# One tile for the untransposed convolution output, its transposes taken block by block, and two steps of the schedule moved

## The chip, the cores and the metric

The kernel runs on one core of a Trainium2 chip. The time is that of the device, in microseconds, for one launch. One further execution was recorded by the hardware profiler, and every row below comes from it. Engine names are those of the profile: PE (matmul) and PEld (its weight loads), DVE, ACT, POOL, and SP, which here only issues DMAs.

## What is computed

```python
# x: (8, 4160, 192), weight: (8 heads, 7 taps)
w   = softmax(weight, axis=-1)                      # per head
out = causal_conv(x_pad, w)                         # each head's 24 columns, 7 taps back in time
t   = out.reshape(33280, 192)
h   = t @ w_in                                      # 192 -> 1024
solu = h * softmax(h)                               # per token
ln  = (solu - mean(solu)) / sqrt(var(solu) + 1e-6) * g_ln
return ln @ w_out                                   # 1024 -> 192
```

## The kernel before

The 33280 tokens are cut in two ways. For the convolution they form 17 **chunks**, mostly of 2080 tokens (half a batch row). For the rest they form 260 **tiles** of 128 tokens, so that a chunk is 16.25 tiles. From tile 8 on, three tiles make a **step** (`three_steps(i)`, where i is the step's first tile), and steps come in the order 8, 11, 14, and so on to 254. A name such as "step 107" means the step of tiles 107, 108 and 109.

The path of a chunk. SP loads it into `xr`. DVE takes partial maxima (L227), and PE adds them over the partitions by a matmul with ones (`add_up`, L99). From that follows the chunk's scale, and from chunk 4 on POOL splits the scaled values into an upper and a lower half-precision part (`halve_steps`, L282, L286 and L289). PE then convolves two heads at a time (`product_of`, L349), in four **sessions** for each chunk. Each session is evacuated by ACT (`upper_part`, L399) and DVE (`lower_part`, L408) into the untransposed tile `y16`, as three blocks of 128 columns: block 0 holds the upper parts of columns 0 to 127, block 2 their lower parts, and block 1 both parts of the last 64 columns. Every block is cut into two parts by time (slots 0 to 9, and 10 to 18). SP transposes a block's part by DMA into one of four buffers in `pad` (`turn`, L450), POOL copies it from there into `ring` (`pack`, L462 and L467), and block 1 is copied once more within SBUF by a DMA into `ring2` (`double`, L481). A tile of tokens reads `ring` and `ring2` as the stationary operand of its first product.

The path of a tile. PE computes `ph` (L861 and the small products of L884 and L896), DVE scales it and takes its minimum (L931), ACT the exponential (L938), DVE the product (L948), ACT the upper half of the result (L956), and POOL the lower half (L968). SP transposes both into `pT` (L970). The second product (L1000) of a tile runs one step or more after its first: at the start of step i for tile i-5, in its middle for i-4, and at its end for i-3.

Each engine works through its own instructions in the order in which the program emits them, and so does SP's DMA queue. The order is written out by hand in `three_steps`, and a table (`plans`) tells in which step a load, a partial maximum, a session, or a group of transposes is emitted. Transposes and `double` go through the list `moves`, from which `move()` takes one at three places of each step: behind the lower half of the step's first tile, behind that of the second, and at the step's end. A `pack` is emitted at the third `move()` after its transpose.

The untransposed output is a fresh tile for each chunk and part, each in a buffer of its own. A new tile can be written only when everything that reads the old one is done:

```python
if first not in self.y16:
    size = NJM - 2 * PW if first else 2 * PW
    self.y16[first] = yp.tile(
        [P, NB, size, P], F16, name=f"y16_{self.ch}_{first}",
        tag=f"y16_{first > 0}", bufs=1,
    )
```

Of the kernel before, what the change touches and what calls it, by code (L numbers as in the profile page):

```python
# [8 lines left out]
F16 = mybir.dt.float16  # L9
# [11 lines left out]
def kernel(  # L21
# [10 lines left out]
    P = 128  # L32
# [9 lines left out]
    NB = 2 * D // P  # L42
    NT = B * S // P
    FIRST = 1024
    PW = 5
# [21 lines left out]
    NJM = max(-(-n // CW) for _, _, n in spans)  # L67
# [4 lines left out]
    cp = ctx.enter_context(tc.tile_pool(name="cp", bufs=1))  # L72
    xp = ctx.enter_context(tc.tile_pool(name="xp", bufs=1))
    yp = ctx.enter_context(tc.tile_pool(name="yp", bufs=2))
# [52 lines left out]
    class Chunk:  # L127
        def __init__(self, ch):
            self.ch = ch
            self.b, self.t0, self.n = spans[ch]  # L130
            self.exact, self.quarter = ch < 4, ch > 2
            self.nw = -(-self.n // CW)
            slots = NWM if self.quarter else self.nw
            self.cuts = list(range(0, slots, PW)) + [slots]
            self.np = len(self.cuts) - 1
            cut = PW if ch == 1 else min(2 * PW, self.nw)
            self.parts = [(0, cut)] + [(cut, self.nw)] * (cut < self.nw)
            self.y16 = {}
            self.raw = [None] * self.np
            self.sums, self.scaled = 0, False  # L140
            assert not self.quarter or (self.nw == NJM and cut == NWM // 2)
            self.peaks = 2 * self.np if ch < 2 else self.np if ch < 4 else 0
            self.part, self.wide = None, {}
# [216 lines left out]
        def at(self, low, col, z, a, b):  # L360


            blk, c = divmod(col + low * (2 * P if col < P else R), P)
            first = self.part_of(a)
            if first not in self.y16:
                size = NJM - 2 * PW if first else 2 * PW
                self.y16[first] = yp.tile(
                    [P, NB, size, P], F16, name=f"y16_{self.ch}_{first}",
                    tag=f"y16_{first > 0}", bufs=1,
                )  # L370
            rows = slice(0, P if self.quarter else CW)
            return self.y16[first][rows, blk, a - first : b - first, c : c + z - col]

        def part_of(self, a):
            return max(y for y, _ in self.parts if y <= a)

        def cut(self, col, width):

# [54 lines left out]
        def turn(self, blk, a, z):  # L433


            first = self.part_of(a)
            got = self.y16[first][:, blk, a - first : z - first, :]
            if self.quarter:
                at = self.pads % 4 * 10 * P
                Chunk.pads += 1  # L440
                self.wide[blk, a] = pad[:, at : at + (z - a) * P].rearrange(
                    "p (w t) -> p w t", t=P
                )
                to = self.wide[blk, a]
            else:
                at = (self.t0 + a * CW) % RING
                assert at + (z - a) * CW <= RING
                got, to = got[0:CW], ring[:, blk, at : at + (z - a) * CW]
                to = to.rearrange("p (w t) -> p w t", t=CW)
            nc.sync.dma_start_transpose(to, got.rearrange("p w d -> p (w d)"))  # L450
# [45 lines left out]
    ring = cp.tile([P, NB * RING], F16, name="ring")  # L496
    ring = ring.rearrange("p (b t) -> p b t", b=NB)
    ring2 = cp.tile([P, RING], F16, name="ring2")
    pad = cp.tile([P, 4 * NFC * D], F16, name="pad")
    raw_out = pad.bitcast(I32).rearrange("p (f t) -> p f t", t=2)  # L500
    gl = cp.tile([P, NFC], F32, name="gl")
# [174 lines left out]
    for e, bank in enumerate(banks):  # L676
        for q in range(2 * per):
            j = q // 2
# [425 lines left out]
    for ch in range(NCH):  # L1104
        lefts.append(left)
        n = (left + spans[ch][2]) // P
# [26 lines left out]
    def sums(c, a, z):  # L1133
        spread_over(a, z, "sum", [(c, h) for j in range(c.np) for h in c.halves(j)])
# [13 lines left out]
    def plans():  # L1148
        c2, c3, c4, c5 = chunks[2:6]
        for i, a, z in ((8, 0, 2), (11, 2, 6), (14, 6, 8)):  # L1150
            at_tile(i, "conv", *[(c2, hg) for hg in c2.groups()[a:z]])
        assert len(c2.groups()) == 8
        at_tile(11, "open", c2)
        for i, part in zip((11, 14), c2.parts):
            at_tile(i, "turn", *[(c2, (blk, *part)) for blk in (1, 0, 2)])
            at_tile(i, "double", (c2, part))
        sums(c2, 6, 8)
        for j, i in ((2, 5), (3, 6)):
            at_tile(i, "load", (c3, j))
        sums(c3, 8, 14)  # L1160
        for j, i in enumerate((10, 12, 14, 16)):
            at_tile(i, "load", (c4, j))
        sums(c4, 16, 22.4)
        for j, i in enumerate((17, 22, 25, 27)):
            at_tile(i, "load", (c5, j))
        for c in chunks[3:]:
            first = next(t.i for t in tiles if t.ch == c.ch)
            s = first - (first - PAIRED) % 3
            steps = [s + 3 * j - 3 * (c.ch > 4) for j in (-5, -4, -3, -2)]
            for i, hg in zip(steps, c.groups()):  # L1170
                at_tile(i, "conv", (c, hg))
            at_tile(steps[2], "open", c)
            p0, p1 = c.parts
            at_tile(steps[2], "turn", *[
                lambda c=c, q=q: turn_piece(c, *q)
                for q in ((0, *p0), (2, *p0), (0, *p1), (1, *p0), (2, *p1), (1, *p1))
            ])
            if c.ch > 5:
                back = next(t for t in tiles if t.ch == c.ch - 3)
                spread_over(back.i, back.i + 0.6 * back.n, "load", [(c, j) for j in range(c.np)])  # L1180
            if c.ch > 4:
                back = next(t for t in tiles if t.ch == c.ch - 3)
                sums(c, back.i + 0.4 * back.n, back.i + 0.9 * back.n)

    class Queue:

# [21 lines left out]
    def follow(c, i):  # L1208

        chain.extend(  # L1210
            (c.add_up, i + 1 + (c.ch > 1)) if f is None else (f, None)
            for f in c.scale_steps()
        )

        def go():
            c.scaled = True
            if c.exact:
                return
            for j in range(c.np):
                queue.put(c.halve_steps(j, quick=False), (c.ch, j))  # L1220

        chain.append((go, None))
# [41 lines left out]
    early, doubles, squares, late, moves = [], [], [], [], []  # L1264
# [173 lines left out]
    def three_steps(i):  # L1438
# [66 lines left out]
            for k, pc, hg in at(n):  # L1505
                k.lower(pc, *hg)

        def move():

            for q in packs:  # L1510
                q[0] -= 1
            while packs and packs[0][0] < 0:
                packs.pop(0)[1]()
            if moves:
                moves.pop(0)()

        def root_squares():
# [142 lines left out]
        if urgent:  # L1660
            for k, q in work["double"]:
                k.double(*q)
        elif start:
            openings()
            doubles.extend(work.get("double", []))
        else:
            opens()
            if not soon:
                turns()
            move()  # L1670
            doubles.extend(work.get("double", []))
        if i == NT - 6:
            ready(b)
# [96 lines left out]
```

## Time and profile before

| | |
|---|---|
| median of two runs | 1278.4 us (1276.75 and 1280.06) |
| profiled execution | 1279.77 us, of which 1278.1 us are the span of the trace |
| PE busy | 1139.7 us, 89% |
| DVE, ACT, POOL busy | 1010.1 (79%), 992.5 (78%), 966.0 (76%) |
| mean granted clock of PE | 0.965 |
| DMA | 231.86 MB, 181 GB/s on average |

Shares of busy time are averages over the whole span. An engine that works through its queue in order can be idle for a while, although its work is waiting, and then the row that ended the idle time tells what it waited for.

### The profile page before, as it was taken

What the parts mean: (1) busy time and instruction counts of PE and PEld (TensorE: products, weight loads), DVE (VectorE), ACT (ScalarE), POOL (GpSimd) and SP (SyncE); (2) the same over time, 40 slices, a digit from 0 to 9 for tenths busy, and PEclk for the clock granted to TensorE, in tenths of its full rate; (3) what the DMA queues carried; (4) which work ended last, traced back from release to release, by engine and by line L of the source; (5) the groups of instructions that cost most, each with busy time, mean ns of one, the idle gap of its engine ahead of it and who ended that gap; (6) DMA issues with size and microseconds to landing.
All of it is one profiled execution on the core that took longest, in us unless ns stands there. A gap on an engine that the chain in (4) does not pass through costs nothing.

```text
span 1278.1 us, 24666 instructions
## 1 busy us (share of the span) xinstructions
PE 1139.7 (89%) x8710; PEld 669.0 (52%) x8710; DVE 1010.1 (79%) x2035; ACT 992.5 (78%) x1788; POOL 966.0 (76%) x862
## 2 busy tenths in 40 slices
PE   5997985969989799998899989798997989989998
PEld 3663542535545455554556545454554646545556
DVE  8876974867878689896789868598895988778777
ACT  7985864867868688786789868597795979779786
POOL 3643376986969679986898959699795998857674
PEclk9899997988999999999999999899998999999999
DMA  8799785995989989998999979899998998979989
GB/s 234 155 184 185 172 172 117 170 209 113 212 149 208 176 174 212 198 199 162 196 203 193 193 161 201 170 179 207 188 187 166 185 207 165 193 152 173 199 157 178
DMA packets 744548, 231.86 MB, mean 181 GB/s; under 512 B 666592, under 2 KB 743336, under 8 KB 744424
## 3 DMA queue, kind: packets, MB, share of 16 engines
q1 hardware_dynamic: 744424, 230.29, 92.6%
q8 instruction: 68, 1.11, 0.4%
q14 instruction: 56, 0.46, 0.1%
HBM read 34.32 MB, written 25.56 MB: 47 GB/s over the span
## 4 chain that ended last, share of the span: by engine, by line
POOL 35%; PE 27%; issue 19%; DMA 8%; ACT 6%; DVE 4%; SPq 1%; POOLq 0%; ACTq 0%; DVEq 0%
POOL p L968 19%; PE po L1000 12%; PE ph L861 11%; DMA pT<-p 6%; POOL ring L467 4%; POOL xs L289 3%; POOL xr L286 2%; POOL t L1071 2%; POOL xs L282 2%; ACT p L956 2%; ACT sq L960 1%; PE ph L896 1%; ACT e L938 1%; DVE ph L931 1%; PE pc L349 1%
## 5 line engine op out<-in xcount | busy, mean ns | idle before, releaser
L968 POOL TENSOR_TENSOR p<-e,p 128x1024 f16<-128x1024 f32 x257 | 548.0, 2136 | 249.8 <-ACT p L956 248.8
L1000 PE MATMUL po<-ohl,pT 128*128 128x192 f16 (+1 forms) x4264 | 559.3, 288 | 73.3 <-DVE y L408 41.1
L1000 PEld LDWEIGHTS <-pT 128*128 128x128 f16 x4264 | 390.5, 99 | 248.7 <-issue 61.2
L861 PE MATMUL ph<-whi,ring 128*128 128x512 f16 x1548 | 423.7, 383 | 13.2 <-POOL ring L467 10.6
L931 DVE TENSOR_SCALAR_CACHE_REDUCE ph<-ph,cv 128x1024 f32<-128x1024 f32 x248 | 319.2, 1288 | 83.6 <-PE ph L896 53.7
L948 DVE SCALAR_TENSOR_TENSOR e<-ph,cv,e 128x1024 f32<-128x1024 f32 x248 | 317.1, 1278 | 22.0 <-ACT e L938 21.3
L938 ACT ACTIVATE e<-ph,sm 128x1024 f32<-128x1024 f32 x260 | 289.6, 1114 | 55.6 <-DVE ph L931 45.0
L861 PEld LDWEIGHTS <-ring 128*128 128x128 f16 x2064 | 193.7, 99 | 235.5 <-issue 30.7
L956 ACT CAST p<-e 128x1024 f16<-128x1024 f32 x257 | 266.5, 1037 | 37.1 <-DVE e L948 34.4
L960 ACT ACTIVATE sq<-e 128x1024 bf16<-128x1024 f32 x260 | 274.2, 1055 | 0.2
L399 ACT ACTIVATE y<-pc 128x432 f16<-128x432 f32 (+5 forms) x130 | 53.9, 475 | 155.2 <-PE pc L349 90.0
L1010 DVE TENSOR_REDUCE raw<-po 128x192 f32<-128x384 f32 x247 | 136.5, 553 | 31.1 <-PE po L1000 28.7
L861 PE MATMUL ph<-wlo,ring 128*128 128x512 f16 x516 | 155.3, 383 | 0.0
L408 DVE SCALAR_TENSOR_TENSOR y<-pc,y 128x432 f16<-128x432 f32 (+5 forms) x130 | 63.3, 532 | 69.0 <-ACT y L399 65.9
L289 POOL TENSOR_TENSOR xs<-xr,xs 128x960 f16<-128x960 f32 x52 | 104.6, 2012 | 1.4
L467 POOL COPY ring<-pad 128x896 f16<-128x896 f16 (+8 forms) x111 | 89.2, 803 | 1.7 <-DMA pad<-y 1.7
L227 DVE TENSOR_REDUCE xa<-xr 128x1 f32<-128x384 f32 x108 | 67.3, 643 | 5.3 <-DMA xr<-in_x_dram 5.3
L896 PE MATMUL ph<-wlo,ring 64*64 64x512 f16 x672 | 51.2, 393 | 19.2 <-DMA ring<-ring 17.1
L286 POOL TENSOR_SCALAR xr<-xr,s 128x960 f32<-128x960 f32 x52 | 55.5, 1067 | 2.6
L1077 ACT ACTIVATE raw<-raw,t 128x192 f32<-128x192 f32 x127 | 56.5, 448 | 0.0
L282 POOL TENSOR_SCALAR xs<-xr,s 128x960 f16<-128x960 f32 x52 | 55.5, 1067 | 0.0
L1071 POOL TENSOR_TENSOR t<-t,mhalf 128x8 f32<-128x8 f32 (+2 forms) x33 | 53.4, 1618 | 2.6
(154 smaller groups left out, 706.5 us busy)
## 6 DMA issues: line engine op xcount, KB each, us to landing
out_dram<-raw SPq DMA_DIRECT2D x127, 192.0 KB, 3.1
xr<-in_x_dram SPq DMA_DIRECT2D x97, 240.0 KB, 4.0
pT<-p SPq DMA_TRANSPOSE x263, 4.6
xr<-in_x_dram SPq DMA_DIRECT2D x6, 480.0 KB, 4.9
xw<-in_x_dram SPq DMA_DIRECT2D x7, 240.0 KB, 4.2
pad<-in_moe_w_out_dram SPq DMA_DIRECT2D x1, 1536.0 KB
ring<-ring SPq DMA_DIRECT2D x12, 120.0 KB, 3.4
ring<-ring SPq DMA_DIRECT2D x10, 140.0 KB, 3.1
```

What stands on the lines that cost most here:

```text
L282: pool.tensor_scalar(h, r, self.s, 1.0, ALU.mult, ALU.mult)
L289: (2.1 * size + 0.2, lambda: pool.tensor_tensor(xl, r, h, ALU.subtract)),
L467: pool.tensor_copy(ring[:, blk, at : at + n * CW].rearrange("p (w t) -> p w t", t=CW), wide[:, w - a : w - a + n, SKIP : SKIP + CW],)
L861: nc.tensor.matmul(bank, lhs, w[:, r, n * 512 : (n + 1) * 512], start=start and j == 0, stop=stop and j == len(ops) - 1,)
L931: dve.tensor_scalar(t.ph, t.ph, t.cv[:, 0:1], None, ALU.mult, ALU.min, accum_out=t.bias)
L938: act.activation(t.e, t.ph, AF.Exp, bias=t.bias, scale=-1.0, accum_out=grp.z[:, g : g + 1])
L948: dve.scalar_tensor_tensor(t.e, t.ph, t.cv[:, 3:4], t.e, ALU.mult, ALU.mult, accum_out=t.grp.s1[:, t.g : t.g + 1],)
L956: act.copy(t.p16[:, :, 0, :], t.halves)
L960: act.activation(junk, t.e, AF.Square, accum_out=t.grp.s2[:, t.g : t.g + 1])
L968: eng.tensor_tensor(t.p16[:, :, 1, :], t.halves, t.p16[:, :, 0, :], ALU.subtract)
L1000: nc.tensor.matmul(t.po[:, 0:n], t.pT[:, a, :], w, start=j == 0, stop=j == len(ops) - 1)
L1010: dve.tensor_reduce(t.grp.raw[:, t.g, :], t.po[:, 0 : 2 * D].rearrange("p (a d) -> p d a", a=2), AX.X, ALU.add,)
```

## The change

Four things change.

1. `y16` becomes one tile for the whole kernel. Nothing is freed between chunks. An instruction that writes into it waits only for those that read or write the same region (chunk 1's second part is put at slots 10 and up, where it lay apart before).
2. The order of a chunk's six transposes changes from (0, first), (2, first), (0, second), (1, first), (2, second), (1, second) to one in which block 1 comes last in both parts, and the `move()` at a step's end takes two entries of the list instead of one.
3. From chunk 4 on, `add_up` may be emitted three tiles later than before, and the partial maxima are spread over an earlier stretch (for chunk 4 the loads, too).
4. Chunk 3's four sessions go from steps 17, 20, 23 and 26 to steps 20, 23, 23 and 26.

```diff
-            self.y16 = {}
...
-            first = self.part_of(a)
-            if first not in self.y16:
-                size = NJM - 2 * PW if first else 2 * PW
-                self.y16[first] = yp.tile(
-                    [P, NB, size, P], F16, name=f"y16_{self.ch}_{first}",
-                    tag=f"y16_{first > 0}", bufs=1,
-                )
             rows = slice(0, P if self.quarter else CW)
-            return self.y16[first][rows, blk, a - first : b - first, c : c + z - col]
+            return y16[rows, blk, self.slots(a, b), c : c + z - col]
+
+        def slots(self, a, b):
+            return slice(a + 5, b + 5) if self.ch == 1 and a >= PW else slice(a, b)
...
-            first = self.part_of(a)
-            got = self.y16[first][:, blk, a - first : z - first, :]
+            got = y16[:, blk, self.slots(a, z), :]
...
+    y16 = cp.tile([P, NB, NJM, P], F16, name="y16")
...
-        for j, i in enumerate((10, 12, 14, 16)):
+        for j, i in enumerate((9, 11, 12, 13)):
             at_tile(i, "load", (c4, j))
-        sums(c4, 16, 22.4)
+        sums(c4, 15, 20)
...
             steps = [s + 3 * j - 3 * (c.ch > 4) for j in (-5, -4, -3, -2)]
+            if c.ch == 3:
+                steps = [20, 23, 23, 26]
...
-                for q in ((0, *p0), (2, *p0), (0, *p1), (1, *p0), (2, *p1), (1, *p1))
+                for q in ((0, *p0), (2, *p0), (0, *p1), (2, *p1), (1, *p0), (1, *p1))
...
-                sums(c, back.i + 0.4 * back.n, back.i + 0.9 * back.n)
+                sums(c, back.i + 0.35 * back.n, back.i + 0.8 * back.n)
...
-            (c.add_up, i + 1 + (c.ch > 1)) if f is None else (f, None)
+            (c.add_up, i + 1 + (c.ch > 1) + 3 * (c.ch > 3)) if f is None else (f, None)
...
-        def move():
+        def move(n=1):
 
             for q in packs:
                 q[0] -= 1
             while packs and packs[0][0] < 0:
                 packs.pop(0)[1]()
-            if moves:
+            for _ in range(min(n, len(moves))):
                 moves.pop(0)()
...
-            move()
+            move(2)
             doubles.extend(work.get("double", []))
```

What this does to the order is shown at three places. Line numbers of the changed kernel are some eight lower (ACT's evacuation is L391 there, the transposes are L441 and L962, POOL's copies L458 and L453).

The first is ACT at the end of step 107, where chunk 9's first session is evacuated (`pc_9_0_0` and `pc_9_0_1` are its two halves). Before, with what each instruction waits for in brackets:

```order
L938 ACTIVATE e_109_6616,z_104_6304<-ph_109_6523,sm_109_6614 128x1024 [waits DVE_49,Pool_49]
L960 ACTIVATE sq_108_6618,s2_104_6306<-e_108_6547 128x1024 [waits Activation_49]
L956 CAST p16_109_6625<-e_109_6616 128x2x512 [waits DMAHW2_49,DVE_49]
L1077 ACTIVATE raw_96_6141<-raw_96_6141,t2_96_5763 128x192
L399 ACTIVATE y16_9_0_6714<-pc_9_0_0_6678 128x10x48 [waits DMAHW3_49,DMAHW5_49,DMAHW0_49,PE_49]
L399 ACTIVATE y16_9_10_6716<-pc_9_0_1_6679 128x9x48 [waits DMAHW2_49,DMAHW3_49,DMAHW0_49,PE_49]
```

And now:

```order
L952 ACTIVATE sq_108_6602,s2_104_6285<-e_108_6527 128x1024 [waits Activation_49]
L262 ACTIVATE xa_10_6183<-xa_10_6183 128x8 [waits DVE_49]
L948 CAST p16_109_6613<-e_109_6600 128x2x512 [waits DMAHW3_49,DVE_49]
L1069 ACTIVATE raw_96_6118<-raw_96_6118,t2_96_5743 128x192 [waits Pool_49]
L391 ACTIVATE y16_76<-pc_9_0_0_6673 128x10x48 [waits PE_49]
L391 ACTIVATE y16_76<-pc_9_0_1_6674 128x9x48 [waits DMAHW1_49,PE_49]
```

Both writes waited for several DMAs, those of all three blocks of chunk 8; now the first of them waits for no DMA, and the second for one, which transposed block 0.

The second place is SP from tile 70 to tile 77, where chunk 6 is transposed (`pad` is the target, `pT` belongs to tiles, `ring2` to `double`). Before:

```order
L970 DMA_TRANSPOSE pT_72_4531<-p16_72_4528 128x16x128
L450 DMA_TRANSPOSE pad_76<-y16_6_10_3914 128x9x128
L970 DMA_TRANSPOSE pT_73_4579<-p16_73_4571 128x16x128
L450 DMA_TRANSPOSE pad_76<-y16_6_0_3912 128x10x128
L1090 DMA out_0_dram<-raw_56_3818 128x2x192
L970 DMA_TRANSPOSE pT_74_4643<-p16_74_4640 128x16x128
L450 DMA_TRANSPOSE pad_76<-y16_6_10_3914 128x9x128
L970 DMA_TRANSPOSE pT_75_4673<-p16_75_4670 128x16x128
L450 DMA_TRANSPOSE pad_76<-y16_6_10_3914 128x9x128
L970 DMA_TRANSPOSE pT_76_4716<-p16_76_4713 128x16x128
L481 DMA ring2_75<-ring_74 64x1120
```

And now:

```order
L962 DMA_TRANSPOSE pT_72_4515<-p16_72_4512 128x16x128
L441 DMA_TRANSPOSE pad_77<-y16_76 128x9x128
L962 DMA_TRANSPOSE pT_73_4563<-p16_73_4555 128x16x128
L441 DMA_TRANSPOSE pad_77<-y16_76 128x10x128
L441 DMA_TRANSPOSE pad_77<-y16_76 128x9x128
L1082 DMA out_0_dram<-raw_56_3809 128x2x192
L962 DMA_TRANSPOSE pT_74_4629<-p16_74_4626 128x16x128
L962 DMA_TRANSPOSE pT_75_4659<-p16_75_4656 128x16x128
L962 DMA_TRANSPOSE pT_76_4706<-p16_76_4703 128x16x128
L472 DMA ring2_75<-ring_74 64x1120
L472 DMA ring2_75<-ring_74 64x960
```

The last two transposes stood behind those of tiles 74 and 75, in the step before the next chunk's first session; now all six stand ahead of tile 74's.

The third place is POOL from tile 106 to tile 108, where chunk 9's last piece is split while chunk 8 is packed (`xr_9_3` and `xs_9` belong to the split, `ring` to the packs, `p16` to tiles). Before:

```order
L286 TENSOR_SCALAR xr_9_3_5278<-xr_9_3_5278,s_9_5750 128x960
L968 TENSOR_TENSOR p16_106_6485<-e_106_6475,p16_106_6485 128x2x512
L467 COPY ring_74<-pad_76 128x1120
L289 TENSOR_TENSOR xs_9_5896<-xr_9_3_5278,xs_9_5896 128x960
L968 TENSOR_TENSOR p16_107_6550<-e_107_6543,p16_107_6550 128x2x512
```

And now:

```order
L960 TENSOR_TENSOR p16_106_6459<-e_106_6449,p16_106_6459 128x2x512
L458 COPY ring_74<-pad_77 128x1120 x2
L281 TENSOR_SCALAR xs_9_6046<-xr_9_3_5259,s_9_5730 128x960
L960 TENSOR_TENSOR p16_107_6530<-e_107_6523,p16_107_6530 128x2x512
L458 COPY ring_74<-pad_77 128x224
L453 COPY ring_74<-pad_77 128x96
L453 COPY ring_74<-pad_77 128x16
L458 COPY ring_74<-pad_77 128x560
L453 COPY ring_74<-pad_77 128x64
L285 TENSOR_SCALAR xr_9_3_5259<-xr_9_3_5259,s_9_5730 128x960
L288 TENSOR_TENSOR xs_9_6046<-xr_9_3_5259,xs_9_6046 128x960
```

The last instruction of the split moved from ahead of tile 107's lower half to behind it, and two more packs stand ahead of it. That holds for chunks 9, 11, 14 and 16, whose `add_up` moved by a step; the other chunks' splits stand where they stood.

## Rows read from the trace of the kernel before

**Rows 1.** Waits, whole span: engine, line, waited for: us in total, times, longest.

```profile
ACT y L399 <- DMA pad<-y: 63.4, 9, 8.8
...
PEld L1000 <- DMA pT<-p: 41.8, 32, 3.1
PE po L1000 <- DVE y L408: 41.1, 11, 7.4
...
ACT y L399 <- DMA ring<-y: 10.8, 1, 10.8
...
PEld po L99 <- ACT xa L263: 9.1, 5, 2.7
```

**Rows 2.** Timeline of ACT in step 107: start, us, what, idle time before it and releaser.

```profile
581.76 0.57 ACT L399 ACTIVATE y<-pc 128x480 f16<-128x480 f32 x1 [1.40 <-PE pc L349]
590.95 0.53 ACT L399 ACTIVATE y<-pc 128x432 f16<-128x432 f32 x1 [8.63 <-DMA pad<-y]
...
591.48 1.11 ACT L938 ACTIVATE e<-ph,sm 128x1024 f32<-128x1024 f32 x1
```

**Rows 3.** Timeline of SP, the same stretch.

```profile
582.60 2.30 SPq L450 DMA_TRANSPOSE pad<-y  x1
...
587.78 1.36 SPq L450 DMA_TRANSPOSE pad<-y  x1
```

**Rows 4.** Timeline of PE, the same stretch.

```profile
580.93 0.78 PE L349 MATMUL pc<-xs,bands 64*64 64x240 f16 x24
...
592.18 5.39 PE L1000 MATMUL po<-ohl,pT 128*128 128x384 f16 x32 [4.95 <-DVE y L408]
```

**Rows 5.** Windows: two steps about a chunk's first session, seven chunks: stretch, us, busy, clock.

```profile
345.30:377.30 32.00, 27.14 (x219) 15.57 (x218) 22.02 (x43) 21.12 (x38) 22.38 (x25) 0.95 0.90 173
...
sum 241.70, PE 192.93 PEld 110.53 DVE 155.37 ACT 148.64 POOL 161.56; mean PE 27.56 PEld 15.79 DVE 22.20 ACT 21.23 POOL 23.08
```

**Rows 6.** The same for the four chunks whose first session comes a step later.

```profile
504.40:531.20 26.80, 25.14 (x218) 15.01 (x217) 22.39 (x48) 21.39 (x38) 24.24 (x27) 1.00 1.05 205
...
sum 108.10, PE 100.87 PEld 60.04 DVE 89.84 ACT 86.05 POOL 85.54; mean PE 25.22 PEld 15.01 DVE 22.46 ACT 21.51 POOL 21.38
```

**Rows 7.** Windows: steps 47 to 230, one quiet step, one stretch of transposes (last: DMA share, GB/s).

```profile
292.60:1159.70 867.10, 796.06 (x6270) 461.83 (x6269) 700.04 (x1394) 686.77 (x1237) 715.18 (x636) 0.98 0.95 183
479.40:491.70 12.30, 12.30 (x82) 6.96 (x80) 11.70 (x23) 12.16 (x25) 11.80 (x11) 1.00 1.09 205
943.60:974.40 30.80, 23.80 (x178) 13.36 (x177) 18.05 (x37) 16.16 (x27) 22.00 (x23) 0.99 1.04 205
```

**Rows 8.** Timeline of ACT at step 17, chunk 3's first session.

```profile
127.08 0.62 ACT L399 ACTIVATE y<-pc,s 128x432 f16<-128x432 f32 x1 [10.83 <-DMA ring<-y]
```

**Rows 9.** Timeline of PE: an undisturbed pair of second products, and that behind step 17.

```profile
105.79 4.08 PE L1000 MATMUL po<-ohl,pT 128*128 128x384 f16 x32
...
128.46 6.82 PE L1000 MATMUL po<-ohl,pT 128*128 128x384 f16 x32 [7.38 <-DVE y L408]
```

**Rows 10.** Timeline of SP at the end of step 23: a transpose of chunk 3, a load of chunk 5.

```profile
173.89 1.83 SPq L450 DMA_TRANSPOSE pad<-y  x1
175.77 1.28 SPq L206 DMA_DIRECT2D xr<-in_x_dram  x2
```

**Rows 11.** Timeline of DVE, the same stretch.

```profile
180.47 0.55 DVE L227 TENSOR_REDUCE xa<-xr 128x1 f32<-128x384 f32 x1 [5.30 <-DMA xr<-in_x_dram]
```

**Rows 12.** Timeline of PE at the first tiles of chunks 3 and 4.

```profile
206.31 1.03 PE L861 MATMUL ph<-whi,ring 128*128 128x512 f16 x2 [9.83 <-POOL ring L467]
...
289.32 1.48 PE L896 MATMUL ph<-wlo,ring 64*64 64x512 f16 x9 [11.70 <-DMA ring<-ring]
```

**Rows 13.** Timeline of POOL in step 107: split, pack, lower half of tile 107.

```profile
569.92 1.07 POOL L286 TENSOR_SCALAR xr<-xr,s 128x960 f32<-128x960 f32 x1
...
573.02 1.13 POOL L467 COPY ring<-pad 128x1120 f16<-128x1120 f16 x1
574.10 2.02 POOL L289 TENSOR_TENSOR xs<-xr,xs 128x960 f16<-128x960 f32 x1
576.07 2.15 POOL L968 TENSOR_TENSOR p<-e,p 128x1024 f16<-128x1024 f32 x1
```

More of the change, by code (lines that the diff above doesn't have):

```diff
@@ L363, in at @@
             blk, c = divmod(col + low * (2 * P if col < P else R), P)
-            first = self.part_of(a)
-            if first not in self.y16:
-                size = NJM - 2 * PW if first else 2 * PW
-                self.y16[first] = yp.tile(
-                    [P, NB, size, P], F16, name=f"y16_{self.ch}_{first}",
-                    tag=f"y16_{first > 0}", bufs=1,
-                )
             rows = slice(0, P if self.quarter else CW)
-            return self.y16[first][rows, blk, a - first : b - first, c : c + z - col]
-        def part_of(self, a):
-            return max(y for y, _ in self.parts if y <= a)
+            return y16[rows, blk, self.slots(a, b), c : c + z - col]
+        def slots(self, a, b):
+            return slice(a + 5, b + 5) if self.ch == 1 and a >= PW else slice(a, b)
         def cut(self, col, width):
```

## Prediction

> **What bounds the kernel now.** I read the page's busy shares first: PE leads with 89%, and from step 47 to step 230 it is busy for 796.06 of 867.10 us [rows 7]. So PE sets the pace of the long middle, and at most 71 us can be won there without taking work from it. A quiet step with a session shows that floor: 12.30 us, all of them PE's [rows 7].
>
> Next I read who waits, longest in total first. Most of those waits cost nothing, since PE doesn't stand behind them. One line does: ACT waited 63.4 us in only nine places for the DMA that transposes `y16` [rows 1], and a wait of up to 8.8 us on ACT, which must give each tile its exponential, reaches PE soon. The timelines of one such place show the whole chain. At 581.76 ACT evacuates the first half of chunk 9's first session. The second half begins 8.63 us later [rows 2], because its buffer is still read by chunk 8's last transpose, issued by SP at 587.78 [rows 3]. Behind that evacuation stands the exponential of tile 110. PE runs out of work and is idle for 4.95 us, until DVE has made its part of the session [rows 4]. Its next 32 matmuls then take 5.39 us, where an undisturbed run of them takes 4.08 [rows 9].
>
> To see what such a place costs in all, I took windows from the first exponential of the step ahead to that of two steps on. Chunks 6, 7, 9, 11, 12, 14 and 16 have their first session in the step behind the last transposes. Their seven windows take 241.70 us, 34.5 each, at a granted clock of 0.95 in the one shown [rows 5]. Chunks 8, 10, 13 and 15 have one step more between, do the same work, and take 108.10 us in four windows, 27.0 each, at a clock of 1.00 [rows 6].
>
> **The change part by part.** The sum is made against the profiled execution, 1279.77 us, which lies 1.4 above the median of the runs.
>
> One tile, block 1 last. The first writes of a chunk's session go to blocks 0 and 2. Both are now transposed before the last two transposes, and these stand one step earlier themselves. So the wait goes in all seven places, and they should take what the other four take: 241.7 - 7 x 27.0 = 52.5 us off. Bounds: PE's own loss, 4.95 + (5.39 - 4.08) = 6.3 in one place, gives 44 in seven; if they became two quiet steps of 12.30, it would be 241.7 - 7 x 24.6 = 69.5. I take 52.5, since the four windows hold the same instructions. What is late next there is the transpose of `p`, for which PE waits 3.1 us at most [rows 1].
>
> Chunk 3's sessions. At step 17 ACT waits 10.83 us for chunk 2's transposes [rows 8], PE is idle for 7.38 and then takes 6.82 for what is 4.08 elsewhere [rows 9]. With the session gone from that step the wait goes, too: 7.4 + 2.7 = 10 us off (bounds 7.4 and 10.8 + 2.7 = 13.5). The session is still done, three tiles later, so that PE's own work neither grows nor shrinks; step 23 has two of them.
>
> The sum over partitions later. PE's weight load waited 9.1 us for it in five places [rows 1]. Two of these lie in the seven windows and are counted. I take 3 off, between 0 and 9.
>
> What it adds, first: SP now has two transposes ahead of chunk 5's last load at the end of step 23. The one of before took 1.83 [rows 10], and DVE already stands for 5.30 us behind that load [rows 11]. One more transpose is 1.8 us, and one more partial maximum stands there, 0.55: 2.5 us on (bounds 1.8 and 3.6).
>
> Second: the split of chunks 9, 11, 14 and 16 ends later on POOL. For chunk 9 it ended at 574.10 + 2.02 = 576.1 [rows 13], 4.8 us before PE wanted it at 580.93 [rows 4]. Now there stand ahead of it in addition tile 107's lower half (2.15), L282's pass (1.07, as L286's), and two packs (1.13, and one of some 1.9 in pieces): about 6.2, so PE waits 1.4 us. Four such chunks give 5.6, if the others have no more room; I take 3 (0 to 8).
>
> Third, the transposes' burst. All six of a chunk now fall from the end of one step to the end of the next, instead of on two steps. Block 1's wait for their `pad` buffers, which POOL must have packed, costs nothing: those packs follow directly on the lower half whose transpose SP issues first, and they take 1.13 each [rows 13]. But every DMA of SP goes through one queue. By the tiles' sizes a step then moves three `pT` of 0.52 MB, six parts of 0.31 and 0.3 of stores: 3.7 MB. In a stretch where SP went from one transpose to the next, the DMAs moved 205 GB/s [rows 7], so that this step needs 18 us and has 12.5. One transpose more (1.8 us) stands ahead of `pT` in that step, two in front of the next step's first tile. PE uses `pT` a step later and so feels only a part. Bounds: nothing, or 3.2 us in each of 13 chunks, 42. The nearest row, PE's 41.8 us of waits for `pT` in 32 places [rows 1], is 1.3 each. I take 8, a small wait in half of the chunks.
>
> The Trainium skill has a rule on this rate ("DMA: Bandwidth & Descriptors", section on latency and other measured facts): DMA transposes with a non-contiguous middle dimension reach 261 GB/s. The trace doesn't agree, at 205; by 261 the burst would last 14 us, and the sum would lose most of its 8.
>
> `double` for chunks 3 and 4. PE waits 9.83 us for a pack and 11.70 for `double` [rows 12]. Both packs keep their place behind tile 31's and tile 46's lower halves, with one pack more ahead of them, which POOL has room for near chunk 3, though hardly near chunk 4. Nothing, within 1.2 us.
>
> Sum: -52.5 - 10 - 3 + 2.5 + 3 + 8 = -52. That is 1227.8 for the profiled execution and **1226.5** for the median, 4.1% faster. (A difference of 2% is about what a measurement of this kernel can tell from no change.)
>
> **The rivals.**
>
> The edges become quiet altogether. For it: the four windows of comparison hold waits for late packs and splits, which earlier packs may end. Then 69.5 instead of 52.5, 13.5 instead of 10, and no burst: 27 us less, about 1200. Against it: POOL and the DMA queue lose the pauses in which they caught up. POOL's 715.18 us of the middle [rows 7] would be 89% of what is left.
>
> The burst costs in full. For it: the DMAs are near their rate already, 183 GB/s over the middle and 205 in the burst [rows 7], and the middle shrinks by 52 us. Against it: no wait for `pT` was above 3.1 us [rows 1]. With 42 instead of 8 the time is about 1260.
>
> Slower than before. The mechanism is the same queue at the same place, the end of a chunk's fourth session: if PE had no reserve on `pT`, a burst's whole excess over a step, 18 - 12.5 = 5.5 us, would fall on PE, and the next step's first sum over partitions, splits and packs would move with it. With the other terms as they are, the change loses when each of 13 chunks costs over (52 + 8) / 13 = 4.6 us, and 5.5 in each give 1226.5 - 8 + 72 = 1290. The longest single wait of 3.1 us [rows 1] speaks against it.
>
> The wait stays. The program still has a DMA semaphore on one of the first writes. If that DMA were late, the seven places would stay as they are: about 1278. Against it: it is a transpose of block 0, issued a whole step earlier than the one waited for now.
>
> **How the numbers follow.** Forecast (1226.5, from 1212 to 1243) 0.62; quiet edges 0.14; burst in full 0.17; wait stays 0.04; slower 0.03. The range leaves out the last two and the outer half of the burst's case, 0.155 in all: 1200 to 1254. Faster by over 2% is below 1252.8: the forecast, the quiet edges and half of the burst's case, 0.85; within 2% 0.13; slower by over 2% 0.02.
>
> **What would show it.** In the profile after, the wait of ACT's evacuation for `pad<-y` is gone or below 5 us in all. The seven windows are near 27 us, with a clock near 1.00. Step 17's evacuation no longer waits for `ring<-y`. The two waits of rows 12 stand as they were, shifted. PE's waits for `pT` may be up to twice the 41.8 us. The prediction is wrong if these have grown to 80 us, or if a new wait for POOL's split stands ahead of L349, at chunks 9, 11, 14 or 16, and is longer than the one removed.

## The result, and the profile after

The changed kernel takes 1239.04 us (1238.38 to 1239.69, two runs) where the kernel before takes 1278.4: 0.969 of its time, 95% interval 0.963 to 0.975. That is 3.1% faster. The forecast was 1226.5, with a range from 1200 to 1254. The profiled execution took 1239.69 us with a span of 1238.0, 40.1 less than the span before.

The waits, whole span, of the kernel after (engine, line, waited for: us in total, times, longest). Its line numbers are 8 to 9 lower: L391 and L400 evacuate a session on ACT and DVE, L441 is `turn`, L458 and L453 `pack`, L472 `double`, L962 the transpose `pT`, L992 the second product.

```profile
PEld L992 <- DMA pT<-p: 64.2, 44, 4.2
...
PE po L992 <- DMA pT<-p: 51.9, 35, 3.9
...
DVE y L400 <- ACT y L391: 13.4, 17, 4.0
```

ACT's wait for `pad<-y`, 63.4 us in nine places [rows 1], is in no row any more, nor is its wait for `ring<-y`, nor PE's 41.1 us for DVE's evacuation. What grew is the wait for `pT`: 41.8 us of PE's weight loads before [rows 1], 64.2 now.

The windows of the kernel after (stretch, its length in us, busy time of each engine, PE's clock, DMA share, GB/s): first the middle from step 47 to step 233, then the first and the sum of the seven windows that stand against [rows 5], the sum of the four that stand against [rows 6], and the four steps that lie just ahead of those four, one of them shown.

```profile
286.40:1119.20 832.80, 787.22 (x6270) 458.27 (x6269) 700.23 (x1394) 687.99 (x1237) 713.24 (x632) 0.99 1.02 191
338.10:365.50 27.40, 25.40 (x218) 14.82 (x217) 21.33 (x41) 21.36 (x38) 27.00 (x32) 1.00 1.08 203
...
sum 209.20, PE 180.50 PEld 104.86 DVE 152.98 ACT 150.13 POOL 193.45; mean PE 25.79 PEld 14.98 DVE 21.85 ACT 21.45 POOL 27.64
...
sum 103.30, PE 100.48 PEld 59.70 DVE 85.00 ACT 85.64 POOL 72.16; mean PE 25.12 PEld 14.92 DVE 21.25 ACT 21.41 POOL 18.04
...
835.10:855.10 20.00, 15.12 (x80) 7.89 (x79) 11.01 (x20) 10.03 (x17) 19.19 (x18) 0.83 1.12 213
...
sum 68.50, PE 54.54 PEld 29.50 DVE 44.58 ACT 40.53 POOL 67.13; mean PE 13.64 PEld 7.38 DVE 11.15 ACT 10.13 POOL 16.78
```

The same four steps in the kernel before, which no row ahead of the prediction shows:

```profile
869.70:884.90 15.20, 12.18 (x79) 6.58 (x78) 11.21 (x20) 9.97 (x16) 14.53 (x12) 1.00 1.15 206
...
sum 53.60, PE 48.13 PEld 26.79 DVE 44.43 ACT 40.21 POOL 52.57; mean PE 12.03 PEld 6.70 DVE 11.11 ACT 10.05 POOL 13.14
```

So the 40.1 us are made up as follows, each from first exponential to first exponential. The seven windows give 241.7 - 209.2 = 32.5, and the four of comparison 108.1 - 103.3 = 4.8. The four steps ahead of the latter take 68.5 - 53.6 = 14.9 back. The other steps of the middle give 867.1 - 832.8 - 32.5 - 4.8 + 14.9 = 11.9, most of it in three steps behind a chunk's sums: step 116 fell from 17.84 to 12.45, 68 from 15.03 to 12.49, 149 from 14.05 to 12.45. Step 14, chunk 3's old wait, fell from 26.14 to 15.94, and the steps from 17 to 47 take 2.6 back. Start and end lose 1.8.

All eleven steps in which a chunk's last transposes are issued (59, 74, 89, 107, 122, 140, 155, 170, 188, 203 and 221, "burst steps" below) are longer than the 12.3 us of a quiet one: 182.9 in sum, 13.9 to 20.0 each. The timeline of PE in the longest, step 170 of the kernel after:

```profile
835.54 2.12 PE L992 MATMUL po<-ohl,pT 128*128 128x384 f16 x16
...
840.96 2.13 PE L992 MATMUL po<-ohl,pT 128*128 128x384 f16 x16 [1.57 <-DMA pT<-p]
846.40 4.02 PE L992 MATMUL po<-ohl,pT 128*128 128x384 f16 x16 [3.31 <-DMA pT<-p]
850.22 1.06 PE L853 MATMUL ph<-whi,ring 128*128 128x512 f16 x2
```

SP in the same step:

```profile
835.37 3.58 SPq L962 DMA_TRANSPOSE pT<-p  x1
839.01 1.34 SPq L441 DMA_TRANSPOSE pad<-y  x1
840.44 0.53 SPq L1082 DMA_DIRECT2D out_dram<-raw  x1
841.08 3.25 SPq L962 DMA_TRANSPOSE pT<-p  x1
844.38 1.36 SPq L441 DMA_TRANSPOSE pad<-y  x1
845.84 2.10 SPq L962 DMA_TRANSPOSE pT<-p  x1
848.05 3.13 SPq L441 DMA_TRANSPOSE pad<-y  x2
```

SP goes from one transfer to the next without a pause, and PE stands still for `pT`. After its stop of 3.31 us PE's 16 matmuls take 4.02 where the same 16 had taken 2.12, and the next products 1.06 where a pair takes 0.59: these run at the lower of the two levels (1.2 for 2.4 GHz). The granted clock was 0.50 from 846.4 to 850.3, and the step's 0.83 is a mean of both levels. So this stop is paid for about twice.

### The profile page after: what moved, and what is told of

The parts are those of the page before. It is cut to its first block, busy times and chain, and to the rows that moved or that the text cites. A ratio compares the mean times of both kernels' runs of the same rounds, so it can differ in the third digit from the quotient of the medians.

```text
span 1238.0 us, 24631 instructions
## 1 busy us (share of the span) xinstructions
PE 1132.0 (91%) x8704; PEld 666.7 (54%) x8704; DVE 1010.7 (82%) x2035; ACT 994.3 (80%) x1788; POOL 966.4 (78%) x862
## 4 chain that ended last, share of the span: by engine, by line
PE 35%; POOL 34%; issue 13%; DMA 9%; DVE 4%; ACT 3%; SPq 1%; POOLq 0%; ACTq 0%; DVEq 0%
PE po L992 16%; POOL p L960 15%; PE ph L853 14%; DMA pT<-p 6%; POOL xs L288 5%; POOL ring L458 4%; POOL xr L285 3%; POOL xs L281 3%; PE ph L888 2%; PE pc L348 2%; POOL t L1063 2%; ACT p L948 1%; DVE ph L923 1%; DMA pad<-y 1%; DVE y L400 1%
## 5 line engine op out<-in xcount | busy, mean ns | idle before, releaser
L992 PE MATMUL po<-ohl,pT 128*128 128x192 f16 (+1 forms) x4264 | 553.2, 286 | 52.8 <-DMA pT<-p 51.9
L992 PEld LDWEIGHTS <-pT 128*128 128x128 f16 x4264 | 386.2, 99 | 225.8 <-DMA pT<-p 64.2
L853 PE MATMUL ph<-whi,ring 128*128 128x512 f16 x1548 | 424.0, 383 | 13.1 <-POOL ring L458 10.5
L948 ACT CAST p<-e 128x1024 f16<-128x1024 f32 x257 | 266.6, 1038 | 35.1 <-DVE e L940 27.1
L391 ACT ACTIVATE y<-pc 128x432 f16<-128x432 f32 (+5 forms) x130 | 53.2, 475 | 98.5 <-PE pc L348 98.4
L458 POOL COPY ring<-pad 128x896 f16<-128x896 f16 (+8 forms) x111 | 87.7, 806 | 0.2 <-DMA pad<-y 0.2
L400 DVE SCALAR_TENSOR_TENSOR y<-pc,y 128x432 f16<-128x432 f32 (+5 forms) x130 | 62.6, 532 | 6.4 <-ACT y L391 3.1
```

Source lines behind the costliest of these rows:

```text
L458: pool.tensor_copy(ring[:, blk, at : at + n * CW].rearrange("p (w t) -> p w t", t=CW), wide[:, w - a : w - a + n, SKIP : SKIP + CW],)
L853: nc.tensor.matmul(bank, lhs, w[:, r, n * 512 : (n + 1) * 512], start=start and j == 0, stop=stop and j == len(ops) - 1,)
L948: act.copy(t.p16[:, :, 0, :], t.halves)
L992: nc.tensor.matmul(t.po[:, 0:n], t.pT[:, a, :], w, start=j == 0, stop=j == len(ops) - 1)
```

## The experiments

The theory to begin with (A): the six transposes of `y`, bunched on SP's queue and in the DMAs, make `pT` late, and cost some 20 us where the prediction had 8. Rivals: pairs of packs on POOL make the lower half of `p` late (B, in another form D: POOL has too much to do in that step), or nothing but PE's own pace is left (C). Later A was split into A1 (the time that SP needs to issue) and A2 (bytes), and F was set against it: the transfers are near their limit in the whole middle, and the burst step is only where it shows.

| kernel | us, median (range) | to before, 95% | burst steps | seven windows | PE's products wait for pT |
|---|---|---|---|---|---|
| before | 1278.4 | 1 | 208.2 | 241.7 | 26.8 |
| changed | 1239.04 | 0.969 (0.963 to 0.975) | 182.9 | 209.2 | 51.9 |
| e1 one by one | 1267.0 (1258.9 to 1269.1) | 0.991 (0.989 to 0.994) | 154.2 | 219.4 | 29.4 |
| e2 two, then one | 1241.8 (1238.9 to 1244.0) | 0.973 (0.971 to 0.975) | 181.7 | 206.9 | 47.0 |
| e3 packs apart | 1238.6 (1234.9 to 1240.1) | 0.971 (0.969 to 0.972) | 180.6 | 206.5 | 46.6 |
| e4 short turns | 1219.4 (1219.3 to 1220.2) | 0.955 (0.954 to 0.957) | 169.4 | 196.3 | 35.6 |
| e5 short packs | 1236.2 (1229.4 to 1237.3) | 0.967 (0.964 to 0.970) | 178.1 | 208.6 | 46.0 |
| e6 three turns | 1273.7 (1271.3 to 1277.1) | 0.998 (0.996 to 1.000) | 170.5 | 211.9 | 30.8 |
| e7 stores on ACT | 1245.9 (1238.3 to 1251.7) | 0.975 (0.972 to 0.978) | 163.1 | 200.7 | 51.7 |
| e8 old sums | 1240.7 (1239.1 to 1246.2) | 0.972 (0.970 to 0.975) | 184.5 | 205.2 | 42.7 |
| e9 short pT ahead | 1214.9 (1211.8 to 1215.6) | 0.951 (0.949 to 0.953) | 156.0 | 194.8 | 31.5 |
| e10 short pT in burst | 1201.2 (1199.4 to 1202.8) | 0.940 (0.938 to 0.942) | 152.1 | 188.3 | 17.4 |
| e11 old turns | 1239.9 (1238.3 to 1242.9) | 0.971 (0.969 to 0.973) | 157.1 | 204.7 | 29.3 |
| e12 tile alone | 1254.9 (1252.8 to 1257.5) | 0.983 (0.981 to 0.986) | 152.9 | 216.2 | 27.2 |

The three columns at the right are from the profiled executions, the steps from first exponential to first exponential; that of e8 was its longest run, 1246.2. The kernel before had medians between 1276.3 and 1278.4 beside these runs, and single runs of one kernel lie up to 13 us apart (e7), so that differences of medians below 5 us are not read.

### One transpose at a time, in the new order (e1)

```diff
-            move(2)
+            move()
```

> The changed kernel, but with one transpose at the end of a step instead of two: the same tile and order, the six transposes over two steps as before. Theory A (the transposes' burst on SP's queue and the DMAs costs about 20 us, not 8): most of that comes back, but the last transpose of block 2 now stands at the end of the fourth session's step, close to the next first session's evacuation, so that ACT waits for it again, 1 to 3 us in seven places. 1222 to 1236, with PE's waits for pT near the 41.8 and 26.8 us of the kernel before (64.2 and 51.9 in the changed one). Theory B (two packs in a row on POOL make the lower half of p late): the same time, since the packs come singly here too. Theory C (no burst: the middle is bound by PE's own pace): 1238 to 1246, slower by what the new wait costs.

Here block 1's first part is packed after the first tiles of chunks 3 and 4 have been read, so that these use old ring rows. It took 1267.0, which no theory had. Two rows of its waits, and one of PE's timeline in step 143:

```profile
PEld L888 <- DMA ring<-ring: 36.6, 12, 4.1
...
PE po L992 <- DMA pT<-p: 29.4, 23, 3.4
```

```profile
734.84 1.49 PE L888 MATMUL ph<-wlo,ring 64*64 64x512 f16 x10 [3.30 <-DMA ring<-ring]
```

`double` of block 1 comes a place too late for a chunk's first tile, and PE waits for it in twelve places. The burst steps, on the other hand, fell to 154.2 us. That looked like theory A. But PE's new stops also gave the transfers time, so e11 had to tell these apart.

### The first two together, then one at a time (e2); packs apart (e3)

```diff
-            move(2)
+            move(2 if work.get("turn") else 1)
```

> The changed kernel, but two transposes only at the end of the third session's step, then one at a time: blocks 0 and 2 are through within the next step, as in the changed kernel, and block 1 follows one at a time. Theory A: the two transposes at the end of the fourth session's step no longer stand ahead of the next pT; 1226 to 1235. Theory B: the same, since the last packs come singly and only the first two in a pair; 1228 to 1236. Theory C: 1237 to 1241.

```diff
-        packs.append([2, pack])
+        age = 1 if (blk, a) == (0, 0) else 3 if blk == 1 and a else 2
+        packs.append([age, pack])
```

> The changed kernel with all its transposes where they are; only the packs are apart, one at each of six places instead of two, one, one and two. Theory A (SP's queue and the DMAs): 1236 to 1241, waits for pT as in the changed kernel, within 5 us. Theory B (pairs of packs on POOL, 3 us ahead of a tile's lower half): 1224 to 1232, POOL's lag behind ACT's cast at the tile after the pair down from 6 us to 3 to 4, waits for pT down by 15 us or more. Theory C: 1237 to 1241.

1241.8 and 1238.6: neither is told from the changed kernel. So it is not the pair of transposes at the end of the fourth session's step, and not the pairs of packs (B).

### Fewer bytes in the transposes of y (e4); less work in the packs (e5)

```diff
+            if self.ch > 4:
+                got, to = got[:, 0:1], to[:, 0:1]
             nc.sync.dma_start_transpose(to, got.rearrange("p w d -> p (w d)"))
```

> The changed kernel, but from chunk 5 on every transpose of y moves only the first of its 7 or 10 windows, so that the wrong columns are packed: as many transposes, waits and packs, a tenth of their bytes. Theory A: the whole price of the y transposes beside pT goes, the lag of SP behind POOL in the fourth session's step falls from 7 to 9 us to about 2, waits for pT fall below 20 us, and the time is 1212 to 1224. Theory B: POOL's pairs stay, 1232 to 1239. Theory C: 1236 to 1240, with the waits for pT gone and the time not.

```diff
             wide = self.wide[blk, a]
+            z = a + 1 if self.ch > 4 else z
```

> The changed kernel, but from chunk 5 on every pack copies only the first of its 7 or 10 windows, so that the ring holds old rows: the transposes of y stay whole and where they are. Theory D (in the step of the burst POOL has three lower halves, four packs, a split and a root, some 17 us of work against 12.4, and so sets its length): 6 us a chunk leave POOL, the step ahead of a first session shrinks from 14 to 20 us to 12.5 to 14, 1215 to 1228. Theory A1 (SP's own issue time: there three pT of 2.3 us, four transposes of y of 1.5, stores and loads, some 17 us as well) and theory A2 (bytes in the DMAs): 1234 to 1240.

Without the bytes 1219.4, 20 us less; with short packs 1236.2, which is 3 less. What e4 takes out costs, and POOL's copies don't, so D falls, too. That is not bytes alone: SP's rows for the 66 transposes of `y` from step 47 to step 233 add up to 94.5 us in e4 and to 104.7 in the changed kernel. The burst steps stayed long even in e4, at 169.4, against the 135 of eleven quiet ones. The wait for `pT` did not fall below the 20 us that A had set; the transposes of `y` are not all of it.

### Half as many transposes (e6); stores on ACT's queue (e7)

```diff
-                at = self.pads % 4 * 10 * P
+                at = self.pads % 2 * 20 * P
...
-        packs.append([2, pack])
+        packs.append([1 if blk == 0 else 2, pack])
...
-                lambda c=c, q=q: turn_piece(c, *q)
-                for q in ((0, *p0), (2, *p0), (0, *p1), (2, *p1), (1, *p0), (1, *p1))
+                nop if q is None else lambda c=c, q=q: turn_piece(c, q, 0, c.nw)
+                for q in (0, 2, None, None, 1)
```

> The changed kernel with three transposes a chunk instead of six, each of a whole block of 17 windows, in two pad buffers instead of four: the same bytes, half the instructions on SP. Theory A1: some 1.2 us per instruction saved, three in each chunk, two of them in the step of the burst; 1218 to 1230. Theory A2: 1236 to 1242. Theory D: 1237 to 1250, since POOL packs 17 windows, 3.4 us, in a row.

Its early pack of the whole of block 0 reaches ring rows that some tiles still have to read, so that those tiles get new ones. PE stops for it in four places, as its waits show:

```profile
PE ph L853 <- POOL ring L453: 43.4, 4, 11.8
```

These stops make the total unreadable. Only the seven windows, which hold none of them, can be read: 211.9 for 209.2, so that half the number of instructions bought nothing there. It didn't relieve SP either: from step 47 to step 233 the 33 whole transposes hold it for 108.0 us where the 66 halves took 104.7. So A1's saving of 1.2 us per instruction never came about, and e6 can't tell A1 from A2.

```diff
-            nc.sync.dma_start(
+            act.dma_start(
                 out[first : first + (z - a) * P, :].rearrange("(g p) d -> p g d", p=P),
```

> The changed kernel with the stores of the output issued on ACT's queue instead of SP's: the same bytes, 0.55 to 1.1 us less on SP for each of some 130 stores. Theory A1: 1 to 1.6 us off a step in which SP is full, in 11 of them, 1222 to 1232, if ACT, 80% busy, has room for the issues. Theories A2 and D: 1237 to 1243.

1245.9, if anything slower. The burst steps did fall, by 19.8 us, and other steps rose. The row of ACT's squares in e7's groups (line, what, count | busy, mean ns | idle time ahead of them and what ended it) shows why:

```profile
L952 ACT ACTIVATE sq<-e 128x1024 bf16<-128x1024 f32 x260 | 274.2, 1055 | 21.0 <-DMA pT<-p 12.5 <-DMA pad<-y 5.7 <-DMA xr<-in_x_dram 2.3
```

and the same row in the changed kernel:

```profile
L952 ACT ACTIVATE sq<-e 128x1024 bf16<-128x1024 f32 x260 | 274.3, 1055 | 0.2
```

Behind the stores ACT stood for 21.0 us. Nor is SP's queue relieved by all of the stores' time: from step 47 to step 233 it loses their 59.6 us, and its rows for `pT` and `y` grow by 44.0. Relief for SP's queue does shorten the burst steps. On an engine with work of its own it is paid for at once.

### The sum over partitions where it was (e8)

```diff
-            (c.add_up, i + 1 + (c.ch > 1) + 3 * (c.ch > 3)) if f is None else (f, None)
+            (c.add_up, i + 1 + (c.ch > 1)) if f is None else (f, None)
```

> The changed kernel without one of its parts: the sum over partitions is three tiles earlier again, as before the change. By the prediction's term, 3 us more (0 to 9): 1239 to 1248. By the steps behind a chunk's sums in the two profiles (step 116: 17.84 before and 12.45 after, 68: 15.03 and 12.49, 149: 14.05 and 12.45), the term was some 9 us: 1246 to 1250.

The wait is back, as e8's row shows:

```profile
PEld po L99 <- ACT xa L262: 10.4, 6, 5.3
```

The median is 1.7 us above that of the changed kernel, less than can be told from none. The 9 us read from three steps were not the price of the later `add_up`: e8 leaves the partial maxima early, and these steps take 39.3 us in it for 37.4 in the changed kernel. With the maxima late as well (e12 below) they take 46.1, for the 38.0 of e11. Nor did PE wait there for the sum. In step 116 of the kernel before it stopped for `pT`:

```profile
625.26 3.73 PE L1000 MATMUL po<-ohl,pT 128*128 128x384 f16 x16 [2.78 <-DMA pT<-p]
```

### Half of pT: ahead of the burst (e9), and in it (e10)

```diff
+        p16 = t.p16.rearrange("p n a f -> p (n a f)")
+        if t.i in short:
+            nc.sync.dma_start_transpose(t.pT[:, 0:NFC, :], p16[:, 0:F])
+        else:
+            nc.sync.dma_start_transpose(t.pT, p16)
...
+    for c in chunks[5:]:
+        first = next(t.i for t in tiles if t.ch == c.ch)
+        s = first - (first - FIRST // P) % 3
+        short.update(range(s - 15, s - 9))
```

(in e10 `range(s - 9, s - 3)`; the second product's 32 matmuls stay, and read the half that is there).

> The changed kernel, but of the six tiles in the two steps ahead of a chunk's transposes of y (chunks 5 to 16), pT takes only the first half of p, so that the second product uses wrong columns for them: 1.6 MB a chunk less in the DMAs, as in the run with short transposes of y, though outside the steps of the burst. Theory A (a local excess: the two steps of the burst need more than a step's time of the DMA queue, elsewhere there is room): 1235 to 1241, steps 89, 122, 170 and 203 together at their 68 us. Theory F (the DMA queue is full throughout, 1.02 of its share even in a quiet step, so that each byte costs wherever it is): 1217 to 1227, and these four steps below 62.

> The same cut of pT, for the six tiles in the two steps in which the transposes of y are made, the burst itself: again 1.6 MB a chunk less. Theory A: as much as with short transposes of y or more, 1213 to 1223, steps 89, 122, 170 and 203 together at 50 to 58 us for 68, and the seven windows at 26 to 28 each. Theory F: the same as the cut in the two steps ahead, 1217 to 1227, with the gain spread over other steps.

The middle, step 47 to step 233, in e9:

```profile
283.10:1091.60 808.50, 778.38 (x6270) 455.17 (x6269) 699.88 (x1394) 687.61 (x1238) 712.86 (x632) 1.00 0.91 173
```

and in e10:

```profile
283.20:1081.60 798.40, 778.17 (x6270) 456.46 (x6269) 699.18 (x1394) 687.27 (x1238) 712.97 (x632) 1.00 0.93 177
```

e9 is the decisive run. Its bytes are taken out where no transpose of `y` is, and by A it should have gained nothing. It gained 24 us, so A in its local form falls. But the burst steps fell by 182.9 - 156.0 = 26.9, thus by all of the gain. This fits a queue whose backlog is carried over steps and shows where PE's reserve of finished `pT` is used up, which is in the burst step. SP's rows of step 170, shown above, begin with a `pT` at 835.37, 0.3 us behind the step's first exponential. In e9 that exponential is at 816.8, and the same `pT` is issued 3.3 us ahead of it:

```profile
813.53 3.69 SPq L966 DMA_TRANSPOSE pT<-p  x1
```

That the backlog is made in every step alike is not shown: no run takes bytes out of the steps farther off. The same cut in the burst itself weighs more: e10 gained 38. Neither time lies in a band that was stated. e9's 1214.9 is below F's, and e10's 1201.2 below those of both theories, although its four steps, 53.8 us, are where A had them. The clock's part can be read here, too. PE's busy time for the same 6270 matmuls fell from 787.22 to 778.38 in e9, at a clock of 1.00 for 0.99: 8.8 us that went on slower matmuls.

### The transposes as before the change (e11); the tile alone (e12)

```diff
-            move(2)
+            move()
...
-                for q in ((0, *p0), (2, *p0), (0, *p1), (2, *p1), (1, *p0), (1, *p1))
+                for q in ((0, *p0), (2, *p0), (0, *p1), (1, *p0), (2, *p1), (1, *p1))
```

> The changed kernel, with one tile for y, but its transposes in the old order and one at a time, (0,2,0,1,2,1) over two steps; what is left of the change beside the tile is chunk 3's sessions, the loads and the later sums. In the run with one transpose at a time in the new order the eleven steps ahead of a first session took 154 us where they take 183 in the changed kernel, and the doubles of block 1, one place too late there, cost 3 to 4 us a chunk. Theory A: with the doubles in time the 29 us stay, less 0 to 2 us in seven places where DVE's lower half now waits for block 2: 1210 to 1226. Theory F: the shorter steps there were only time that the late doubles gave the DMA queue; 1234 to 1243. If ACT waited for these transposes whatever the tile (the tile is not the cause), 1265 to 1280.

1239.9: the same as the changed kernel, and what F expected. The burst steps fell to 157.1, but the steps just behind them rose from 146.7 to 162.8 us, since DVE now waits where ACT did before the change. In e11's waits:

```profile
PEld L992 <- DMA pT<-p: 46.4, 39, 4.6
...
DVE y L400 <- DMA pad<-y: 26.0, 7, 4.6
```

e12 is e11 with chunk 3's sessions, the loads and the sums undone as well: the kernel before with nothing new but the one tile.

> The kernel before, with one part of the change alone: one tile for y, and nothing else (transposes in the old order one at a time, chunk 3's sessions, loads and sums as before). By the run of the changed kernel with the old turns (1239.9), plus chunk 3's 8 to 10 and the sums' 2: 1248 to 1254, the seven windows near the 204.7 of that run, ACT's waits for pad gone, and DVE's waits for it near 26 us in seven places. If the order and the pairs of transposes carry the gain together with the tile, 1262 to 1275; if the tile carries all of it, 1238 to 1244.

1254.9, 0.983 of the time before (0.981 to 0.986), within a microsecond of the band that e11 gave; but the seven windows take 216.2, not 204.7. One tile alone takes 21.5 us off. ACT waits for no `pad` any more, DVE does for 26.9 us in seven places. Chunk 3's sessions, the loads and the sums are worth the 15.0 us between e12 and e11. With some 10 for chunk 3 (step 14 takes 25.45 in e12 and 15.94 in e11) about 5 are left for loads and sums.

## Why the prediction was right, and where it was off

**The wait of ACT** went, as forecast, and one tile is the cause (e12). With a tile for each part, each half of the evacuation had to wait until all three blocks of its part had been transposed, and the second half [rows 2] thus for the last transpose of all; in one tile it waits only for its own block.

**52.5 us from seven windows** was too much: they gave 32.5. The step that failed is "they should take what the other four take". The other four windows begin a step later than the seven, behind the burst, and hold none of it. The burst step of those four chunks lay just outside the comparison, and it grew, too, by 14.9.

**The burst, +8 within 0 to 42,** is the term that was mis-sized. Measured against the same 27.0 us a window it is 209.2 - 189.0 + 14.9 = 35.1 us, 3.2 in each of eleven chunks: the upper bound's 3.2 a chunk, for which the prediction shows no working, and which the rival of the burst in full took. The value of 1.3 a wait came from waits for `pT` in the kernel before [rows 1]. There the transfers had pauses where the change removes the waits: a DMA share of 0.90 in the window about such a wait [rows 5] and of 1.05 in one without [rows 6]; in the middle 0.95 [rows 7], and 1.02 after. The rival's argument, that the DMAs are near their rate and the middle shrinks, was right and got 0.17. By the rate of 261 GB/s that the Trainium skill states for DMA transposes with a non-contiguous middle dimension ("DMA: Bandwidth & Descriptors", section on latency and other measured facts) this term would have been smaller still; no run shows whether the transposes here are of that kind. The middle after moved 191 GB/s at a share above 1, so the measured 205 was the one to use.

**The four windows and the other steps** gave 4.8 and 11.9. The first stands in no term; it is a part of what the rival of the quiet edges foresaw. The second holds the sums' 3 (0 to 9): with `add_up` alone undone (e8) they are 1.7, with the partial maxima and loads, too (e12), about 5, so the term stands within its bounds and its size stays open. The prediction's reading of [rows 1] was wrong here: three of the five waits, not two, lie in the seven windows (at 448.3, 827.5 and 983.3), and the two outside add up to 2.2 us. The 9.5 us of the three steps came by way of `pT`, which no term had.

**Chunk 3, -10,** was right: 10.2 in step 14. **Chunk 5's load, +2.5:** the steps from 17 to 47 lost 2.6, though not for the reason given. DVE's wait for the load is 5.38 us, as before the 5.30 of [rows 11]; step 23 with its two sessions grew by 2.9, and step 17 by 3.1, in which DVE now stands for a load for 3.81 us (at 132.64) where it did not before. **The split, +3,** cost nothing. No row shows PE's L348 waiting for POOL. For chunk 9 POOL's last pass ends at 563.04 and PE begins at 564.66 (rows below), 1.6 us of room where there were 4.8 before [rows 4, 13]: it shrank by half of the 6.2 us reckoned. **The two waits of rows 12** stand, at 10.5 and 11.6 us.

The timelines of POOL and PE in the kernel after, ahead of chunk 9's first session:

```profile
561.03 2.01 POOL L288 TENSOR_TENSOR xs<-xr,xs 128x960 f16<-128x960 f32 x1
```

```profile
564.66 0.78 PE L348 MATMUL pc<-xs,bands 64*64 64x240 f16 x24
```

**The sum.** Forecast -52, measured -40.1: 20.0 lost in the seven windows, 6.9 more in the burst steps of the four chunks than the 8 allowed in all, and 1.8 at start and end, given back in part by the 4.8, by some 9 in the other steps and by the split's 3. That the time lies within the forecast's 1212 to 1243 is in part luck, since some 14 us came back in places that no term named. (The rival of the quiet edges adds up to 17 + 3.5 + 8 = 28.5 us, not 27, and so to 1198, just below the stated range.) Pairs and order of the transposes, to which the prediction tied its first term, are worth nothing that was measured (e11 and the changed kernel, 1239.9 and 1239.0): the old order leaves DVE a wait for block 2, the new one gives PE a longer wait for `pT`.

**What stays open.** How the cost divides between SP's time and the bytes, since no run takes the one, leaves the other, and spoils nothing. e4 took 10.2 us of SP's rows for `y` beside its bytes, and its middle is 16.5 us shorter. e9 and e10 took both together, too: a halved `pT` holds SP for 1.3 us, a whole one for 2.3 in the median. e7 moved SP's stores alone, got part of their time back in longer rows of `pT`, and spoiled ACT. No run has the stores on a queue that costs nothing. None of the runs that do all of the work is measurably faster than the changed kernel; e3 is level with it.

## What to carry to other kernels

A wait that is removed gives time back only as far as the next resource has room for it. So hold the bytes of a whole period (here a chunk) against the rate that the trace shows, and the share of that queue against 1, before counting the gain. A stall also serves others as a pause: waits read beside it are too short for the kernel without it. And a window that is to stand for "the same without the wait" must hold the same work; here it began just behind the step in which the rest of the price fell due.

## What was not expected of the hardware

A `pT` halved in the two steps ahead of the burst shortens the burst steps nearly as much as one halved within it (e9 26.9 us, e10 30.8), though the whole gain is less (24 for 38). A transpose of a tenth of the bytes holds SP hardly less, 1.43 us in the mean for 1.59, while a whole block (e6) holds it for 3.27. e4's timeline shows one in step 170 beside the 1.34 above:

```profile
826.36 1.22 SPq L443 DMA_TRANSPOSE pad<-y  x1
```

while `pT` with half of its bytes falls from over 2 us to this, in e10:

```profile
816.62 1.27 SPq L964 DMA_TRANSPOSE pT<-p  x1
```

And a store on ACT's queue takes 0.38 us of issue, but up to 3.38 us stood idle ahead of it:

```profile
986.95 0.38 ACTq L1082 DMA_DIRECT2D out_dram<-raw  x1
987.37 1.06 ACT L952 ACTIVATE sq<-e 128x1024 bf16<-128x1024 f32 x1 [3.38 <-DMA pT<-p]
```
